# DMA transposes in place of TensorE transposes from the third group on, in a fused attention and MLP kernel

## The chip, the cores and the metric

The kernel runs on one core of one Trainium2 chip. The metric is device time in microseconds (us); the time before is 234.18 us, the median of three runs (233.75 to 235.13).

## What is computed

The input is q, k and v for 4 batches, 8 heads, 768 positions and a head dimension of 64, with one decay factor per head. Decayed linear attention gives a matrix of 3072 rows (batch and position) by 512 (head and head dimension), and an MLP follows, with the activation h times tanh(softplus(h)), called Mish. Cut to what matters:

```
for b in range(nb):                       # blocks of positions, in order
    intra = (qb @ kb.T) * Dmask           # lam ** (i - j) on and below the diagonal
    inter = (qb * lam_pow) @ kv_state
    out[b] = intra @ vb + inter
    kv_state = lam_block * kv_state + (kb * rev_pow).T @ vb
x = out as (batch * position, head * head_dim)      # 3072 x 512
h = x @ w_in                                        # 3072 x 2048
result = (h * tanh(softplus(h))) @ w_out            # 3072 x 512, float32
```

## The kernel before, in words

The positions are cut into NG = 6 groups of C = 128, numbered n = 0 to 5 here as in the code. A group holds one chunk of 128 positions of each of B = 4 batches; chunk i is batch i % 4 of group i // 4. Each chunk is worked on in two halves of four heads, so a group has eight halves.

**Attention of one half** is three pieces. `att_a` (L211) makes two transposes on TensorE: `pk` from the decayed k, `ktil` (L220, two matmuls of 128 columns against an identity), and `pq` from q (L223, two more). With group 1 and later it also issues `att_kv` (L187, two matmuls `pv` of 128 columns, k transposed times v) ahead of what follows. VectorE multiplies `pq` by the powers of the decay into `qT` (L230), and ScalarE copies `pk` into the zero-padded `kz` in two instructions of 64 partitions (L234). `att_w` (L200) updates the state of the half: VectorE adds (`raw`, L208), GpSimd multiplies (L209). `att_s` (L243) makes the scores `pS` in four matmuls (L248), and VectorE masks them into `sb` (L252). `att_o` (L255) makes `pO` from `sb`, v, and from group 1 on the state (L266, L270), and ScalarE copies it into `xt` (L273). The PSUM tiles pk, pq, pS and pO have one buffer each.

**The MLP of one group** is 32 units of four matmuls of 512 columns: 16 units `mm1_unit` (L316; `ph`, then Mish on ScalarE into `hsg`, L323), and 16 units `mm2_unit` (L327; `po`, four units for each chunk, then ScalarE copies to `osb`, L340, and SyncE (SP) issues the store, L342).

**The order** is written out by hand, and each engine runs its instructions in that order. The attention of group 0 comes first, alone. Loop n then emits the 32 units of group n's MLP with the 24 pieces of group n+1's attention between them: a0, a1, s0, then a, s, o of consecutive halves. In loop 0 the pieces stand four at a time after units 25 to 30 (units counted from 0); in loops 1 to 4 one piece stands after each unit from 7 to 30. Loop 5 has the MLP alone.

**Loads.** k, q and v are loaded from HBM and cast to 16 bits by DMAs that GpSimd (POOL) issues (L69, L73, L76), 128 KB of result each. `scale_k` (L174) multiplies k by its decay into `ktil`: on VectorE for group 0 and for chunk 8, on GpSimd for the others (L177). The weights are loaded between chunk 3 and chunk 4. The loads of group 2 (chunks 8 to 11) are issued at the end of loop 0, those of later groups in the second half of each chunk's `att_a`, one group ahead.

Of the kernel before, what the change touches and what calls it, by code (L numbers as in the profile page):

```python
# [21 lines left out]
def kernel(  # L22
# [10 lines left out]
    nc = tc.nc  # L33
    B, H, S, D = q.shape
    C = 128
    NG = S // C
    JP = H // 2
# [5 lines left out]
    MID = C // 2 - 1  # L43
    NVB = 8
    NKB = 4

    ctx.enter_context(tc.manual_schedule())
# [7 lines left out]
    qn = [None] * (NG * B)  # L55
# [7 lines left out]
    def load_k(i):  # L63
        if i < 2:
            kn[i] = const.tile([128, H, D], F32, name=f"kn{i}")
            nc.sync.dma_start(out=kn[i], in_=chunk_rows(k, i))
            return
        kn[i] = loads.tile([128, H, D], F16, name="kn", tag="kn")
        nc.gpsimd.dma_start(out=kn[i], in_=chunk_rows(k, i))  # L69
# [26 lines left out]
    def load_chunk(i):  # L96
        load_k(i)
        load_q(i)
        load_v(i)
# [54 lines left out]
    for hp in range(2):  # L154
        rs = slice(64 * hp, 64 * hp + 64)
# [3 lines left out]
    lq = const.tile([128, JP, C], F32, name="lq")  # L159
# [9 lines left out]
    ktil = {}  # L169

    class Half:
        pass

    def scale_k(i):  # L174

        t = work.tile([128, H, D], F16, name="ktil", tag="ktil", bufs=6)
        (nc.vector if i < B or i == 2 * B else nc.gpsimd).tensor_tensor(  # L177
            out=t, in0=kn[i], in1=bc(lk, 2, D), op=ALU.mult)
        ktil[i] = t


    wst = [
# [4 lines left out]
    def att_kv(s, spare):  # L187

        n, b, hf = s.n, s.b, s.hf
        i = n * B + b  # L190
        pv = ps.tile([128, 2, 128], F32, name="pv", tag=spare, bufs=2)
        for p in range(2):
            j = 2 * hf + p
            nc.tensor.matmul(  # L194
                pv[:, p, :].rearrange("p (a e) -> p a e", a=2), s.kp[p],
                vz[i % NVB][:, 2 * j : 2 * j + 2, 0:D], start=True, stop=True,
            )
        s.pv = pv

    def att_w(s):  # L200
        n, b, hf = s.n, s.b, s.hf
        w_new = wst[b][hf][(n + 1) % 2]
        lb = lbm[:, 2 * hf : 2 * hf + 2, :]
        if n == 0:
            nc.vector.tensor_tensor(out=w_new, in0=s.pv, in1=lb, op=ALU.mult)
        else:
            raw = work.tile([128, 2, 128], F32, name="raw", tag="raw", bufs=3)
            nc.vector.tensor_tensor(out=raw, in0=s.pv, in1=wst[b][hf][n % 2], op=ALU.add)  # L208
            nc.gpsimd.tensor_tensor(out=w_new, in0=raw, in1=lb, op=ALU.mult)  # L209

    def att_a(s):  # L211

        n, b, hf = s.n, s.b, s.hf
        i = n * B + b
        pk = ps.tile([128, 2, C], F32, name="pk", tag="pk")
        pq = ps.tile([128, 2, C], F16, name="pq", tag="pq")
        s.kp = [ktil[i][:, 4 * hf + 2 * p : 4 * hf + 2 * p + 2, :].rearrange("p h c -> p (h c)")
              for p in range(2)]
        for p in range(2):
            nc.tensor.matmul(pk[:, p, :], s.kp[p], ident, start=True, stop=True)  # L220
        for p in range(2):
            j = 2 * hf + p
            nc.tensor.matmul(  # L223
                pq[:, p, :], qn[i][:, 2 * j : 2 * j + 2, :].rearrange("p h c -> p (h c)"),
                ident, is_transpose=True, start=(p == 0), stop=(p == 1),
            )
        if 0 < n < NG - 1:
            att_kv(s, s.spare)
        s.qT = work.tile([128, 2, C], F16, name="qT", tag="qT", bufs=5)
        nc.vector.tensor_tensor(out=s.qT, in0=pq, in1=lq[:, 2 * hf : 2 * hf + 2, :], op=ALU.mult)  # L230
        s.kz = kz[s.seq % NKB]
        for hp in range(2):
            rs = slice(64 * hp, 64 * hp + 64)
            nc.scalar.activation(s.kz[rs, :, hp, :], pk[rs], AF.Copy)  # L234
        if n > 0:
            if n < NG - 1:
                att_w(s)
            if hf == 0 and i + 1 < s.loaded:
                scale_k(i + 1)
            if hf == 1 and n > 1 and i + B < NG * B:  # L240
                load_chunk(i + B)

    def att_s(s):  # L243

        psS = ps.tile([128, 4, C], F32, name="pS", tag="pS")
        for p in range(2):
            for hp in range(2):
                nc.tensor.matmul(  # L248
                    psS[:, 2 * p + hp, :], s.kz[:, p, hp, :], s.qT[:, p, :], start=True, stop=True,
                )  # L250
        s.sb = work.tile([128, 4, C], F16, name="sb", tag="sb", bufs=4)
        nc.vector.tensor_tensor(  # L252
            out=s.sb, in0=psS, in1=bc(maskT, 1, 4), op=ALU.mult)

    def att_o(s):  # L255

        n, b, hf = s.n, s.b, s.hf
        i = n * B + b
        if xt[n] is None:
            xt[n] = work.tile([128, JP, GT], F16, name="xt", tag="xt", bufs=2)  # L260
        psO = ps.tile([128, 2, C], F32, name="pO", tag="pO")
# [81 lines left out]


    scale_k(0)
    first_halves = att_halves(0)
    nh = len(first_halves)
# [17 lines left out]
    for hp in range(2):  # L365
        rs = slice(64 * hp, 64 * hp + 64)
        nc.vector.tensor_copy(lbm[rs, :, rs], bc(lbc[rs, :], 2, D))
    for n in range(NG):
        units = [(mm1_unit, (n, ni)) for ni in range(NKI)]
        units += [(mm2_unit, (n, b, part)) for b in range(B) for part in range(WS)]  # L370
        pieces = []
        if n + 1 < NG:
            pieces = att_pieces(n + 1)

        first = 24 if n == 0 else len(units) - 2 - len(pieces)
        room = len(units) - 2 - first
        per = len(pieces) / max(room, 1)
        for u, (fn, args) in enumerate(units):
            fn(*args)
            if n == 0 and 2 <= u < 2 + nh:  # L380
                att_kv(first_halves[u - 2], "po")
                att_w(first_halves[u - 2])
            if u == first - 3 and pieces:
                scale_k((n + 1) * B)
            left = len(units) - 2 - u
            while pieces and u >= first and len(pieces) > per * left:
                f2, s = pieces.pop(0)
                s.spare = "po" if u < NKI - 1 else "ph"
                f2(s)
        for f2, s in pieces:  # L390
            f2(s)
        if n == 0:
            for i in range(2 * B, 3 * B):
                load_chunk(i)


# [28 lines left out]
```

## Time and profile before

| | before |
|---|---|
| median of three runs | 234.18 us |
| the profiled execution's own time | 233.51 us |
| its span, first to last instruction | 231.7 us |
| granted TensorE clock | 1.000 |
| TensorE matmuls busy | 220.0 us (95%) |
| weight loads, beside the matmuls | 120.8 us (52%) |
| VectorE / ScalarE / GpSimd busy | 74.8 / 128.0 / 111.5 us |

The profiled execution is 1.81 us longer than its span and 0.67 us shorter than the median. Matmuls overlap in the trace: a matmul of 512 columns is shown with 379 ns, but four of them start within 0.86 us. So durations on TensorE are read from the starts of consecutive rows, not from busy time. The chain of work that ended last names, at each moment, what the end of the program depended on.

### The profile page before, as it was taken

The page shows a single profiled execution, that of the slowest core. Times are in us where ns is not written, and L with a number is a line of the kernel's source. Part 1 is how long each engine was busy: PE and PEld are TensorE (multiplying, and loading weights), DVE is VectorE, ACT ScalarE, POOL GpSimd, SP SyncE. Part 2 cuts the span into 40 slices and gives each one's busy share as a digit, 9 for nine tenths or more (in the row PEclk, how much of TensorE's full clock was granted, in tenths as well). Part 3 has the DMA queues.
Part 4 walks back from the last instruction along what each step waited for, and adds up shares of the span by engine and source line. Part 5 has one row for each costly group of instructions (what it writes and reads, how often), then busy time and mean ns, then how long its engine had stood idle before and what let it go on. Part 6 is the DMA issues. An engine that isn't in the chain of part 4 may idle for free.

```text
span 231.7 us, 3918 instructions
## 1 busy us (share of the span) xinstructions
PE 220.0 (95%) x1541; PEld 120.8 (52%) x1541; DVE 74.8 (32%) x159; ACT 128.0 (55%) x275; POOL 111.5 (48%) x139
## 2 busy tenths in 40 slices
PE   7797999789899999999999999999999999999993
PEld 2474544466445555545555545555545555544441
DVE  7784410277215443014433114433103323100000
ACT  5884662355577553477554477544478554476121
POOL 7992435766999865219865309865800000000000
PEclk9999999999999999999999999999999999999999
DMA  7999999921999978906988905998900011200112
GB/s 114 137 163 206 205 206 159 194 42 36 102 168 98 77 88 91 152 0 43 75 91 94 156 0 37 73 97 94 155 3 3 0 45 51 89 0 3 45 52 84
DMA packets 82722, 20.44 MB, mean 88 GB/s; under 512 B 75536, under 2 KB 79632, under 8 KB 82704
## 3 DMA queue, kind: packets, MB, share of 16 engines
q0 software_dynamic: 77024, 13.37, 73.3%
q1 hardware_dynamic: 5680, 6.82, 8.3%
q8 instruction: 12, 0.20, 0.4%
q14 instruction: 6, 0.05, 0.1%
HBM read 27.27 MB, written 6.29 MB: 145 GB/s over the span
## 4 chain that ended last, share of the span: by engine, by line
PE 77%; DMA 9%; POOL 7%; ACT 3%; issue 2%; DVE 1%; POOLq 0%; ACTq 0%
PE po L334 35%; PE ph L311 28%; DMA wout_84<-in_moe_w_out_dram 9%; PE pS L248 4%; PE pO L270 3%; PE pk L220 2%; PE pO L266 2%; PE pq L223 1%; POOL qn L73 1%; ACT kz_151 L234 1%; PE pv L194 1%; ACT hsg L323 1%; POOL kn L69 1%; DVE sb L252 1%; ACT xt L273 1%
## 5 line engine op out<-in xcount | busy, mean ns | idle before, releaser
L323 ACT ACTIVATE hsg<-ph 128x512 f16<-128x512 f32 x96 | 57.2, 597 | 25.1 <-PE ph L311 24.8
L334 PEld LDWEIGHTS <-hsg 128*128 128x128 f16 x384 | 34.6, 98 | 29.1 <-issue 0.5
L230 DVE TENSOR_TENSOR qT<-pq,lq 128x256 f16<-128x256 f16 x48 | 20.3, 424 | 90.3 <-PE pq L223 90.1
L252 DVE TENSOR_TENSOR sb<-pS,maskT 128x512 f16<-128x512 f32 x48 | 33.1, 689 | 22.4 <-PE pS L248 22.2
L273 ACT ACTIVATE xt<-pO 128x256 f16<-128x256 f32 x48 | 18.4, 382 | 31.3 <-PE pO L270 31.0
L340 ACT ACTIVATE osb<-po 128x512 f32<-128x512 f32 x24 | 14.3, 597 | 28.8 <-PE po L334 28.6
L73 POOL DMA_DIRECT2D qn<-in_q_dram x24 | 21.7, 905 | 6.9 <-DMA win_78<-in_moe_w_in_dram 2.8
L334 PE MATMUL po<-wout_84,hsg 128*128 128x512 f16 x96 | 24.6, 379 | 0.2 <-DMA wout_84<-in_moe_w_out_dram 0.2
L334 PE MATMUL po<-wout_81,hsg 128*128 128x512 f16 x96 | 24.6, 379 | 0.0
L334 PE MATMUL po<-wout_82,hsg 128*128 128x512 f16 x96 | 24.6, 379 | 0.0
L334 PE MATMUL po<-wout_83,hsg 128*128 128x512 f16 x96 | 24.6, 379 | 0.0
L311 PE MATMUL ph<-xt,win_79 128*128 128x512 f16 x96 | 23.9, 379 | 0.0
L311 PE MATMUL ph<-xt,win_80 128*128 128x512 f16 x96 | 23.7, 379 | 0.0
L311 PE MATMUL ph<-xt,win_77 128*128 128x512 f16 (+2 forms) x104 | 22.2, 363 | 1.1 <-DMA win_77<-in_moe_w_in_dram 0.6
L69 POOL DMA_DIRECT2D kn<-in_k_dram x22 | 20.4, 929 | 5.2 <-DMA win_77<-in_moe_w_in_dram 1.9
L311 PE MATMUL ph<-xt,win_78 128*128 128x512 f16 x96 | 22.0, 379 | 0.0
L177 POOL TENSOR_TENSOR ktil<-kn,lk 128x512 f16<-128x512 f16 x19 | 19.9, 1057 | 0.0
L220 PEld LDWEIGHTS <-ktil 128*128 128x128 f16 x96 | 9.2, 98 | 15.7 <-issue 5.2
L220 PE MATMUL pk<-ident,ktil 128*128 128x128 f16 x96 | 13.3, 221 | 3.9 <-ACT kz_151 L234 1.7
L311 PEld LDWEIGHTS <-win_77 128*128 128x128 f16 x104 | 9.7, 98 | 11.7 <-DMA win_77<-in_moe_w_in_dram 0.8
L311 PEld LDWEIGHTS <-win_78 128*128 128x128 f16 x96 | 9.2, 98 | 10.4
L223 PE MATMUL pq<-ident,qn 128*128 128x128 f16 x96 | 13.3, 220 | 0.0
(167 smaller groups left out, 268.5 us busy)
## 6 DMA issues: line engine op xcount, KB each, us to landing
out_dram<-osb SPq DMA_DIRECT2D x24, 256.0 KB, 2.0
qn<-in_q_dram POOLq DMA_DIRECT2D x24, 128.0 KB, 4.8
kn<-in_k_dram POOLq DMA_DIRECT2D x22, 128.0 KB, 3.7
win_77<-in_moe_w_in_dram POOLq DMA_DIRECT2D x1, 512.0 KB, 7.6
win_78<-in_moe_w_in_dram POOLq DMA_DIRECT2D x1, 512.0 KB, 10.1
win_79<-in_moe_w_in_dram POOLq DMA_DIRECT2D x1, 512.0 KB, 12.0
win_80<-in_moe_w_in_dram POOLq DMA_DIRECT2D x1, 512.0 KB, 13.7
wout_81<-in_moe_w_out_dram POOLq DMA_DIRECT2D x1, 512.0 KB, 15.5
```

The source lines that it names most:

```text
L69: nc.gpsimd.dma_start(out=kn[i], in_=chunk_rows(k, i))
L73: nc.gpsimd.dma_start(out=qn[i], in_=chunk_rows(q, i))
L177: (nc.vector if i < B or i == 2 * B else nc.gpsimd).tensor_tensor(out=t, in0=kn[i], in1=bc(lk, 2, D), op=ALU.mult)
L220: nc.tensor.matmul(pk[:, p, :], s.kp[p], ident, start=True, stop=True)
L223: nc.tensor.matmul(pq[:, p, :], qn[i][:, 2 * j : 2 * j + 2, :].rearrange("p h c -> p (h c)"), ident, is_transpose=True, start=(p == 0), st ...
L230: nc.vector.tensor_tensor(out=s.qT, in0=pq, in1=lq[:, 2 * hf : 2 * hf + 2, :], op=ALU.mult)
L252: nc.vector.tensor_tensor(out=s.sb, in0=psS, in1=bc(maskT, 1, 4), op=ALU.mult)
L273: nc.scalar.activation(dst, psO, AF.Copy)
L311: nc.tensor.matmul(ph_t[ni][:, lo:hi], win[ni // w][:, kc, (ni % w) * 128 : (ni % w) * 128 + 128], xt[n][:, kc, lo:hi], start=(kc == 0), s ...
L323: nc.scalar.activation(hsg[n][:, ni, :], ph_t.pop(ni), AF.Mish)
L334: nc.tensor.matmul(po, hsg[n][:, ki, b * C : (b + 1) * C], wout[part][:, kk, :], start=(ki == 0), stop=(ki == NKI - 1),)
L340: nc.scalar.activation(osb, po, AF.Copy)
```

## The change

From group 2 on (`NT = 2`), TensorE no longer transposes. A new function `turn(i)` scales chunk i's k as before and has SP issue two DMA transposes of a whole chunk, both from SBUF to SBUF: of q into `qraw` and of `ktil` into `kraw`, four buffers each. `att_a` then reads these: VectorE makes `qT` out of `qraw`, and VectorE, not ScalarE, copies `kraw` into `kz`. The PSUM of pk and pq, free now, gives pS and pO a second buffer each. `scale_k` of chunk 8 goes from VectorE to GpSimd.

The times at which things are issued move too. The pieces of group 1's attention stand thinner in loop 0, from unit 22 on instead of 25 (a table gives the pieces after each unit). In the later loops they stand one unit earlier, from unit 6 on. Eight of the twelve loads of group 2 are issued one at a time, one in each `att_a` of group 1; the other four, and `turn(8)`, follow at the end of loop 0. At the start of each later loop `turn` is called for the next group's second chunk, and from loop 2 on for its first; the third and fourth follow in the first halves of the first and second chunk.

```diff
+    def turn(i):
+        scale_k(i)
+        for src, name, to in ((qn, "qraw", qraw), (ktil, "kraw", kraw)):
+            to[i] = work.tile([128, JP, C], F16, name=name, tag=name, bufs=4)
+            nc.sync.dma_start_transpose(out=to[i], in_=src[i].rearrange("p h c -> p (h c)"))
+    ahead = [
+        (lambda f=f, i=i: f(i)) for i in range(2 * B, 3 * B) for f in (load_k, load_q, load_v)
+    ]
...
+        if n >= NT:
+            if n < NG - 1:
+                att_kv(s, s.spare)
+            nc.vector.tensor_tensor(
+                out=s.qT, in0=qraw[i][:, 2 * hf : 2 * hf + 2, :], in1=lqh, op=ALU.mult)
+            for hp in range(2):
+                rs = slice(64 * hp, 64 * hp + 64)
+                nc.vector.tensor_copy(s.kz[rs, :, hp, :], kraw[i][rs, 2 * hf : 2 * hf + 2, :])
+            if n < NG - 1:
+                att_w(s)
+            if hf == 0 and i + 2 < s.loaded:
+                turn(i + 2)
+            if hf == 1 and i + B < NG * B:
+                load_chunk(i + B)
+            return
...
         if n > 0:
-            if n < NG - 1:
-                att_w(s)
             if hf == 0 and i + 1 < s.loaded:
                 scale_k(i + 1)
-            if hf == 1 and n > 1 and i + B < NG * B:
-                load_chunk(i + B)
+            att_w(s)
+            ahead.pop(0)()
...
-        psS = ps.tile([128, 4, C], F32, name="pS", tag="pS")
+        psS = ps.tile([128, 4, C], F32, name="pS", tag=("pS", "pk")[s.seq % 2 if s.n >= NT else 0])
...
-        first = 24 if n == 0 else len(units) - 2 - len(pieces)
+        if n == 0:
+            room = dict(zip(range(22, 31), (1, 1, 2, 3, 3, 4, 4, 4, 2)))
+            if n > 0 and pieces and u == 0:
+                if n > 1:
+                    turn((n + 1) * B)
+                turn((n + 1) * B + 1)
...
         if n == 0:
-            for i in range(2 * B, 3 * B):
-                load_chunk(i)
+            turn(2 * B)
+            while ahead:
+                ahead.pop(0)()
```

On TensorE, this is the second half of chunk 8 (group 2) in loop 1, before the change. Rows name the line, the operation, and out<-in; the number behind a name tells buffers apart.

```order
L220 LDWEIGHTS ktil_953
L220 MATMUL pk_1003<-ident_87,ktil_953 128x128
L220 LDWEIGHTS ktil_953
L220 MATMUL pk_1003<-ident_87,ktil_953 128x128
L223 LDWEIGHTS qn_910
L223 MATMUL pq_1004<-ident_87,qn_910 128x128
L223 LDWEIGHTS qn_910
L223 MATMUL pq_1004<-ident_87,qn_910 128x128
L194 LDWEIGHTS ktil_953
L194 MATMUL pv_1009<-vz0_69,ktil_953 128x128
L194 LDWEIGHTS ktil_953
L194 MATMUL pv_1009<-vz0_69,ktil_953 128x128
```

The same half on TensorE with the change, with the matmul rows of the MLP on both sides of it (line 205 is line 194 of before, line 341 is line 311).

```order
L341 LDWEIGHTS win1_78
L341 MATMUL ph_999<-xt_693,win1_78 128x512
L205 LDWEIGHTS ktil_922
L205 MATMUL pv_1006<-vz0_69,ktil_922 128x128
L205 LDWEIGHTS ktil_922
L205 MATMUL pv_1006<-vz0_69,ktil_922 128x128
L341 LDWEIGHTS win2_79
L341 MATMUL ph_1020<-xt_693,win2_79 128x512
```

Four matmuls and four weight loads of the half are gone, and the piece now stands one unit earlier.

GpSimd during group 1's attention in loop 0, before: `ktil` of chunks 4 to 7 alternates with the state updates `w`, and the loads of group 2 begin behind the last of them.

```order
L177 TENSOR_TENSOR ktil_600<-kn_129,lk_179 128x512
L209 TENSOR_TENSOR w000_196<-raw_635,lbm_195 128x256
L177 TENSOR_TENSOR ktil_638<-kn_134,lk_179 128x512
L209 TENSOR_TENSOR w010_198<-raw_653,lbm_195 128x256
L209 TENSOR_TENSOR w100_200<-raw_676,lbm_195 128x256
L177 TENSOR_TENSOR ktil_679<-kn_139,lk_179 128x512
L209 TENSOR_TENSOR w110_202<-raw_714,lbm_195 128x256
L209 TENSOR_TENSOR w200_204<-raw_752,lbm_195 128x256
L177 TENSOR_TENSOR ktil_755<-kn_144,lk_179 128x512
```

The same place on GpSimd with the change, up to the same `ktil` of chunk 7.

```order
L181 TENSOR_TENSOR ktil_584<-kn_129,lk_179 128x512
L181 TENSOR_TENSOR ktil_619<-kn_134,lk_179 128x512
L220 TENSOR_TENSOR w000_196<-raw_621,lbm_195 128x256
L70 DMA kn_624<-in_k_dram 128x8x64
L220 TENSOR_TENSOR w010_198<-raw_646,lbm_195 128x256
L74 DMA qn_649<-in_q_dram 128x8x64
L181 TENSOR_TENSOR ktil_676<-kn_139,lk_179 128x512
L220 TENSOR_TENSOR w100_200<-raw_678,lbm_195 128x256
L77 DMA vz0_69<-in_v_dram 128x8x64
L220 TENSOR_TENSOR w110_202<-raw_715,lbm_195 128x256
L70 DMA kn_718<-in_k_dram 128x8x64
L181 TENSOR_TENSOR ktil_752<-kn_144,lk_179 128x512
```

Chunk 5 is scaled one place earlier, and four loads of group 2 stand ahead of the scaling of chunk 7; four more follow, and then the scaling of chunk 8. On SP, where before only the 24 stores followed the first loads, the order is now: the four stores of group 0, the eight transposes of group 2 (q, then k, for each chunk), the four stores of group 1, the eight transposes of group 3, and so on; the eight stores of groups 4 and 5 come last.

More of the change, by code (lines that the diff above doesn't have):

```diff
@@ L45 @@
     NKB = 4
+    NT = 2
     ctx.enter_context(tc.manual_schedule())
@@ L172 @@
         pass
+    kraw = {}
+    qraw = {}
     def scale_k(i):
         t = work.tile([128, H, D], F16, name="ktil", tag="ktil", bufs=6)
-        (nc.vector if i < B or i == 2 * B else nc.gpsimd).tensor_tensor(
+        (nc.vector if i < B else nc.gpsimd).tensor_tensor(
             out=t, in0=kn[i], in1=bc(lk, 2, D), op=ALU.mult)
         ktil[i] = t
+    def turn(i):
[3 more added lines that the diff above has]
+            nc.sync.dma_start_transpose(out=to[i], in_=src[i].rearrange("p h c -> p (h c)"))
     wst = [
@@ L214, in att_a @@
         i = n * B + b
+        lqh = lq[:, 2 * hf : 2 * hf + 2, :]
+        s.qT = work.tile([128, 2, C], F16, name="qT", tag="qT", bufs=5)
+        s.kz = kz[s.seq % NKB]
+        s.kp = [ktil[i][:, 4 * hf + 2 * p : 4 * hf + 2 * p + 2, :].rearrange("p h c -> p (h c)")
+                for p in range(2)]
+        if n >= NT:
[13 more added lines that the diff above has]
+            return
         pk = ps.tile([128, 2, C], F32, name="pk", tag="pk")
         pq = ps.tile([128, 2, C], F16, name="pq", tag="pq")
-        s.kp = [ktil[i][:, 4 * hf + 2 * p : 4 * hf + 2 * p + 2, :].rearrange("p h c -> p (h c)")
-              for p in range(2)]
         for p in range(2):
@@ L373 @@
             pieces = att_pieces(n + 1)
-        first = 24 if n == 0 else len(units) - 2 - len(pieces)
-        room = len(units) - 2 - first
-        per = len(pieces) / max(room, 1)
+        if n == 0:
+            room = dict(zip(range(22, 31), (1, 1, 2, 3, 3, 4, 4, 4, 2)))
+        else:
+            room = {u: 1 for u in range(len(units) - 2 - len(pieces), len(units) - 2)}
         for u, (fn, args) in enumerate(units):
@@ L382 @@
                 att_w(first_halves[u - 2])
[L383 to L386, printed above, removed]
+            if n == 0 and u == 18:
+                scale_k(B)
+            if n > 0 and pieces and u == 0:
+                if n > 1:
+                    turn((n + 1) * B)
+                turn((n + 1) * B + 1)
+            for _ in range(room.get(u, 0)):
                 f2, s = pieces.pop(0)
```

10 lines of the change are left out of this document (3 added, 7 removed).

## Prediction

> **What bounds the kernel now.** I read the page first, for the share of each engine and for the chain that ended last.
>
> ```profile
> span 231.7 us, 3918 instructions
> PE 220.0 (95%) x1541; PEld 120.8 (52%) x1541; DVE 74.8 (32%) x159; ACT 128.0 (55%) x275; POOL 111.5 (48%) x139
> PE 77%; DMA 9%; POOL 7%; ACT 3%; issue 2%; DVE 1%; POOLq 0%; ACTq 0%
> ```
>
> TensorE (PE) is busy nearly throughout and holds 77% of the chain; no other engine passes 55%. The share is an average, so I took the chain in order of time next (start, duration, what).
>
> ```profile
> 16.75 20.95 DMA wout_84<-in_moe_w_out_dram
> ...
> 60.55 6.92 PE ph L311 x32
> ...
> 95.64 6.92 PE ph L311 x32
> ...
> 165.81 6.92 PE ph L311 x32
> ...
> 200.11 13.81 PE ph L311 x64
> ```
>
> Until 16.75 + 20.95 = 37.7 us the last weight load sets the pace. From there the chain is TensorE's. The rows "ph L311 x32" mark where loops 1, 2 and 4 begin: loop 1 lasts 95.64 - 60.55 = 35.09 us, loop 4 200.11 - 165.81 = 34.30, and the last MLP 231.7 - 200.11 = 31.6. Those 32 matmuls are eight units of the MLP, so a unit is 6.92 / 8 = 0.865 us. To see whether a loop has room, I read the timeline of TensorE where loop 3 comes to the first two halves of group 4's attention.
>
> ```profile
> 137.47 0.28 PE L220 MATMUL pk<-ident,ktil 128*128 128x128 f16 x2
> 137.58 0.28 PE L223 MATMUL pq<-ident,qn 128*128 128x128 f16 x2
> 137.69 0.28 PE L194 MATMUL pv<-vz_69,ktil 128*128 128x128 f16 x2
> 137.80 1.03 PE L311 MATMUL ph<-xt,win_79 128*128 128x512 f16 x4
> 138.98 0.27 PE L220 MATMUL pk<-ident,ktil 128*128 128x128 f16 x2 [0.15 <-ACT kz_151 L234]
> ```
>
> Each pair of 128-column matmuls delays the next start by 0.11 us, so one costs 0.055. A loop with state updates then needs 32 x 0.865 + 8 x 16 x 0.055 = 27.7 + 7.0 = 34.7 of its 35.1 us: loops 1 to 4 are streams of matmuls with holes of 0.4 us. What is taken off TensorE there comes off the time, unless something else is late.
>
> **The transposes taken off TensorE.** Groups 2 to 5 lose 4 groups x 8 halves x 4 matmuls = 128, at 0.055 us: 7.04 us. The weight loads that go with them run beside matmuls.
>
> **A wait that goes with them.** The last row above starts at 138.98, though the unit before it ends at 137.80 + 0.86 = 138.66: the second half's `pk` waits 0.32 us for ScalarE to empty the only buffer. That is about the 0.4 us missing above, once in each of four loops: 1.28 us. With the change the half begins with `pv`, which has two buffers. What is late next is VectorE, which empties them.
>
> ```profile
> L230 DVE TENSOR_TENSOR qT<-pq,lq 128x256 f16<-128x256 f16 x48 | 20.3, 424 | 90.3 <-PE pq L223 90.1
> L252 DVE TENSOR_TENSOR sb<-pS,maskT 128x512 f16<-128x512 f32 x48 | 33.1, 689 | 22.4 <-PE pS L248 22.2
> L208 DVE TENSOR_TENSOR raw<-pv,w_210 128x256 f32<-128x256 f32 x2 | 0.8, 415 | 0.0
> L156 DVE COPY lnp<-lnb 64x4 f32<-64x4 f32 x2 | 0.5, 245 | 0.6 <-ACT lnb L149 0.5
> L367 DVE COPY lbm<-lbc 64x256 f32<-64x256 f32 x2 | 0.9, 471 | 0.1
> ```
>
> VectorE gains two copies of 64x256 a half. No row has them from SBUF in 16 bits; the copies shown bound them at 245 and 471 ns, and the larger shape is the nearer. A half then costs VectorE at most 0.42 + 0.94 + 0.42 + 0.69 = 2.5 us, against 3 units and 12 small matmuls on TensorE, 3.25 us. So they hide, and without that cover each half would cost what is over. ScalarE loses its two copies, which were off the path. GpSimd's extra `scale_k` of chunk 8 stands behind group 1's attention.
>
> **The transposes as DMAs.** No DMA in this trace transposes, so I bound them. The first two are from the DMA view of 57 to 72 us, when loads run at full rate; the others are the page's, and SP's timeline where loop 1 begins.
>
> ```profile
> q0 software_dynamic: 12465, 1.57, 164.5%
> ...
> out_dram<-osb SPq DMA_DIRECT2D x1, 256.0 KB, 4.5
> ...
> q1 hardware_dynamic: 5680, 6.82, 8.3%
> out_dram<-osb SPq DMA_DIRECT2D x24, 256.0 KB, 2.0
> ...
> 61.21 0.33 SPq L342 DMA_DIRECT2D out_dram<-osb  x1
> ```
>
> Occupancy first. SP's queue moved 6.82 MB in 8.3% of 231.7 us, so 128 KB at that rate takes 0.37 us. The loads moved 12465 packets in 15 us, 831 a microsecond; a load of 128 KB with rows of 64 elements has 128 x 8 = 1024 of them, so 1.23 us. Were a transpose cut into 65536 pieces of 2 bytes at the same packet rate, it would be 79 us. I take 0.4 to 1.2, because the order shows one DMA for each 128x512 block, as for a load. A loop's 8 transposes, 12 loads and 4 stores are then at most 9.6 + 14.8 + 3.0 = 27.4 us of some 33: the DMA engines keep up.
>
> Latency next. A store lands 2.0 us after its issue, 4.5 among loads. Take chunk 12, whose transposes stand behind the last store of loop 1. That store is issued 61.21 - 60.55 = 0.66 us after a loop begins and holds SP 0.33 us; q's transpose then holds SP by 0.33 to about 1.2 us (its occupancy), and k's lands 2.0 to 4.5 us after its issue, so 3.3 to 6.7 us after the loop began. It is needed by s0, behind units 0 to 8 and two `pv` pairs, 9 x 0.865 + 0.22 = 8.0, less `qT` and the two copies, 1.36: 6.6 us. So it is in time by 3.3 us or late by 0.1; I take in time. In loops 2 to 4 the second chunk has those five units more, the third and fourth are asked for nine units or more ahead of their first piece. The q transposes wait only for loads that landed a loop before. What is queued behind a waiting transpose on SP is transposes, and then the stores of the group, which begin 13 units later. GpSimd, whose `ktil` the k transposes wait for, is free where loops 2 to 4 begin. In loop 1 it still issues group 2's loads: by the rows of the next part chunk 8's `ktil` ends 7.8 us (four `w`, four loads, one scaling) after chunk 7's, at 61.7, and chunk 9's 4.9 us later, at 66.6. Loop 1 begins at 59.7, so chunk 8 lands by 4.0 to 6.5 us in, with 6.6 allowed, and chunk 9 by 8.9 to 11.4, with 11.9 allowed (s2 stands five units and 1.0 us of pieces behind s0).
>
> **The first attention in loop 0.** Here TensorE has holes. First its rows, then GpSimd's.
>
> ```profile
> 41.20 1.03 PE L334 MATMUL po<-wout_84,hsg 128*128 128x512 f16 x4
> ...
> 43.78 0.27 PE L220 MATMUL pk<-ident,ktil 128*128 128x128 f16 x2
> ...
> 53.81 0.27 PE L220 MATMUL pk<-ident,ktil 128*128 128x128 f16 x2
> ```
>
> ```profile
> 42.37 1.08 POOL L177 TENSOR_TENSOR ktil<-kn,lk 128x512 f16<-128x512 f16 x1
> 45.04 0.73 POOL L209 TENSOR_TENSOR w_196<-raw,lbm 128x256 f16<-128x256 f32 x1 [1.59 <-DVE raw L208]
> ...
> 52.56 1.05 POOL L177 TENSOR_TENSOR ktil<-kn,lk 128x512 f16<-128x512 f16 x1
> 57.53 0.95 POOL L69 DMA_DIRECT2D kn<-in_k_dram  x1
> ```
>
> From 43.78 to 60.55 TensorE has 6 units and 24 pieces, 5.2 + 7.0 = 12.2 us of work in 16.8. With the change a0 stands behind unit 22, at 41.20. Chunk 4's `ktil` still ends at 42.37 + 1.08 = 43.45, since the loads of group 1 stand ahead of it on GpSimd; TensorE idles 2.3 us and owes three more units, 2.6 us. It gets them back from the holes up to a6, which needs chunk 7's `ktil`. GpSimd now reaches that by 45.04 + 4 x 0.73 + 4 x 0.95 + 2 x 1.05 = 53.9, against 52.56 + 1.05 = 53.6. So a6 starts at about 53.9, as it does now (53.81), and from it on stand three units, 2.6 us, and a6 to o7, 48 small matmuls, 2.6: 5.2 us, where it now takes 60.55 - 53.81 = 6.7. Some holes stay: o7 waits for ScalarE to empty the one pO, a7's scores for its copies. I allow 0.7 us and take a gain of 0.8. Bounds: 1.5 if no hole stays, a loss of 1 if the loads and `w` reach a6 two places later.
>
> **The sum**, on the profiled execution: 233.51 - 7.04 - 1.28 - 0.8 = 224.4 us. The median stood 0.67 above it: 225.1 us.
>
> **The rivals.**
>
> Transposes go one at a time, and SP's queue becomes the bound (slower). Mechanism: 32 transposes with a price T each, from 60.4 us on, and each waits for the one before it. The last must be there for a6 of loop 4; behind that stand 0.9 us of VectorE, 10 units and 36 small matmuls, 10.6 us, and the last MLP, 31.6. The span is 60.4 + 32 T + 43.1, which passes 231.7 from T = 4.0 us on. By the landing time of the store among loads, 4.5, the span is 247.5 and the time 247.5 + 1.81 + 0.67 = 250 us. For it: nothing here shows a transpose. Against: a store's transfer and landing, 0.37 and 2.0, lie far below 4.0. Chance 0.15, the case of 79 us each (2.6 ms in all) within it.
> The Trainium skill (VectorE: DVE Perf Modes, "The three transpose paths") has a 128x128 transpose of 16 bits at 390 ns on TensorE and 1309 ns by DMA, and so speaks against the change. Four such blocks in a row are an estimate of 5.2 us for one of these DMAs; by that rule the span would be 270 us. No run here shows it, and TensorE's 0.055 us for such a block against the page's 390 ns shows that its figures are not prices in a stream.
>
> The first chunk of each group is late, or loop 0 loses. If `kraw` lands 1.3 us late in four loops, 5.2 us of the gain go: 230.3. If GpSimd's interleaved loads push a6 by 2 us, it is 227. Both still gain. Chance 0.11.
>
> The matmuls were covered anyway (no change, 234.2). TensorE would have to wait elsewhere for the same time, on VectorE above all. Against: it shows 2.5 us a half against 3.25, and the loops have 0.4 us of holes. Chance 0.06.
>
> **How the numbers follow.** No change means within 0.5% (1.2 us), which is about what a measurement of this kernel can tell. The forecast, 223.3 to 227.5, has 0.68; with the late cases faster has 0.79, same 0.06, slower 0.15. The range goes from 223.3 (loop 0 gains 0.7 more, the loops lose their last 0.1 us of holes each, and the run stands as far below its median as the profiled one did, 0.7) to 231.5, the late case with 1.2 us of scatter, and leaves out the last two, 0.2.
>
> **What would show it.** In the new profile loops 1 to 3 should last about 33.0 us and loop 4 about 32.2; loop 1 should begin at about 59.7; DVE's `qT` from `qraw` should wait for TensorE's order of work or nothing, not for a DMA. A row of VectorE or TensorE that waits for `kraw` or `qraw` at a loop's start for more than its slack, or SP with transposes back to back over a loop, proves me wrong, and the sign then hangs on T against 4.0 us.

## The result, and the profile after

The changed kernel takes 228.02 us (median of 4 runs, 227.86 to 228.25) against 233.97 us for the kernel before, in runs on the same chip: a ratio of 0.974, 95% interval 0.970 to 0.977. That is 2.6% faster, where 3.9% was forecast; 2.9 us of the forecast gain are missing. The profiled execution took 227.86 us, 5.65 less than that of before.

The page of the changed kernel, its span, the busy time of the engines and the shares of the chain:

```profile
span 226.0 us, 3703 instructions
...
PE 211.8 (94%) x1413; PEld 113.0 (50%) x1413; DVE 99.6 (44%) x222; ACT 105.8 (47%) x211; POOL 113.5 (50%) x140
...
PE 73%; DMA 12%; POOL 9%; DVE 2%; issue 1%; SPq 1%; ACT 1%; POOLq 0%; ACTq 0%; DVEq 0%
```

128 matmuls are gone (1541 to 1413), ScalarE is 22 us less busy and VectorE 25 us more. The share of DMA in the chain has grown from 9% to 12%: a transfer has come onto the path. The chain in order of time shows which (start, duration, what):

```profile
61.75 1.30 SPq L190
63.18 7.01 DMA kraw<-ktil
72.24 0.98 DVE kz_152 L243
...
96.32 6.04 PE ph L341 x28
...
129.30 6.04 PE ph L341 x28
...
162.29 7.77 PE ph L341 x36
...
194.38 13.81 PE ph L341 x64
```

The new link is one transpose, `kraw` of chunk 8 at the start of loop 1, with 7.01 us from issue to landing. Behind it the chain is TensorE's alone. The rows "ph L341" mark where loops 2, 3 and 4 and the last MLP begin (the chain puts these starts 0.16 to 0.17 us later than TensorE's timeline does): loop 2 lasts 129.30 - 96.32 = 32.98 us, loop 3 32.99, loop 4 32.09. TensorE's timeline shows the places where it stood still, first in loop 0, then in loop 1:

```profile
43.63 0.28 PE L254 MATMUL pk<-ident,ktil 128*128 128x128 f16 x2 [2.12 <-POOL ktil L181]
...
53.64 0.28 PE L254 MATMUL pk<-ident,ktil 128*128 128x128 f16 x2
...
57.30 0.38 PE L278 MATMUL pS<-qT,kz_154 128*128 128x128 f16 x4 [0.78 <-DVE sb L282]
...
59.36 0.22 PE L296 MATMUL pO<-qT,w_211 128*128 128x128 f16 x1 [0.47 <-ACT xt L303]
...
60.55 3.62 PE L341 MATMUL ph<-xt,win_77 128*128 128x512 f16 x16
...
67.68 1.03 PE L341 MATMUL ph<-xt,win_79 128*128 128x512 f16 x4
70.56 0.60 PE L278 MATMUL pS<-qT,kz_151 128*128 128x128 f16 x4 [1.84 <-DVE kz_151 L243]
70.99 1.03 PE L341 MATMUL ph<-xt,win_79 128*128 128x512 f16 x4
...
72.83 0.22 PE L278 MATMUL pS<-qT,kz_152 128*128 128x128 f16 x1
73.27 0.34 PE L278 MATMUL pS<-qT,kz_152 128*128 128x128 f16 x3 [0.22 <-DVE kz_152 L243]
```

The unit at 67.68 ends at 68.55, and s0 starts at 70.56: 2.0 us late, with 0.2 more in the slow `pS` itself and 0.4 at the next half's `kz_152`. That is 2.6 us, and loop 1 lasts 35.6 us where 33.0 were forecast. The table has, from the profiled execution of each kernel below, when the last weight load lands (its issue plus its time to landing), where loop 1 begins on TensorE's timeline, and how long the loops are.

| kernel | last weight load lands | loop 1 begins | loop 1 | loop 2 | loop 3 | loop 4 |
|---|---|---|---|---|---|---|
| before | 37.70 | 60.39 | 35.08 | 35.09 | 35.08 | 34.31 |
| changed | 37.85 | 60.55 | 35.60 | 32.99 | 32.99 | 32.09 |
| e1 late loads | 37.36 | 60.07 | 32.99 | 32.98 | 32.99 | 32.09 |
| e2 copies on ScalarE | 37.20 | 59.91 | 37.26 | 33.69 | 33.69 | 33.19 |
| e3 single pS and pO | 37.72 | 60.44 | 36.63 | 32.99 | 32.98 | 32.09 |
| e4 loop 0's table alone | 37.68 | 60.74 | 35.09 | 35.08 | 35.09 | 34.31 |
| e5 loop 0 early | 37.17 | 60.43 | 32.99 | 32.99 | 32.98 | 32.10 |
| e6 loads together | 36.91 | 59.62 | 36.20 | 32.99 | 32.98 | 32.09 |
| e7 third group on TensorE | 37.73 | 60.45 | 35.09 | 32.99 | 32.98 | 32.09 |
| e8 transposes twice | 37.29 | 60.00 | 35.78 | 33.18 | 32.98 | 32.10 |
| e9 loop 0 early, later table | 37.20 | 57.99 | 32.99 | 32.99 | 32.99 | 32.09 |
| e10 late loads again | 36.52 | 59.23 | 32.99 | 32.99 | 32.98 | 32.10 |

Loops 2 to 4 give 2.10 + 2.09 + 2.22 = 6.4 us; loop 1 takes 0.5 back and its start 0.2: 5.7 us, which is the difference of the two profiled executions (5.65). The start of loop 1 scatters with the last weight load, and a difference of 0.2 us there says nothing by itself. Counted from that landing, loop 1 begins 22.69 us later in the kernel before, and 22.70 in the changed kernel (22.70 to 22.72 in all eight versions with its table for loop 0): loop 0 gained nothing and lost nothing. The question for the experiments is why neither loop 1 nor loop 0 gains anything.

### The profile page after: what moved, and what is told of

Its sections match the earlier page's. It is cut to its first block, busy times and chain, and to the rows that moved or that the text cites. A ratio compares the mean times of both kernels' runs of the same rounds, so it can differ in the third digit from the quotient of the medians.

```text
span 226.0 us, 3703 instructions
## 1 busy us (share of the span) xinstructions
PE 211.8 (94%) x1413; PEld 113.0 (50%) x1413; DVE 99.6 (44%) x222; ACT 105.8 (47%) x211; POOL 113.5 (50%) x140
## 4 chain that ended last, share of the span: by engine, by line
PE 73%; DMA 12%; POOL 9%; DVE 2%; issue 1%; SPq 1%; ACT 1%; POOLq 0%; ACTq 0%; DVEq 0%
PE po L364 34%; PE ph L341 26%; DMA wout_84<-in_moe_w_out_dram 9%; PE pS L278 4%; PE pO L300 4%; DMA kraw<-ktil 3%; PE pO L296 2%; POOL qn L74 2%; PE pv L205 1%; POOL kn L70 1%; DVE kz_152 L243 1%; DVE sb L282 1%; SPq L190 1%; ACT osb L370 1%; POOL ktil L181 0%
## 5 line engine op out<-in xcount | busy, mean ns | idle before, releaser
L239 DVE TENSOR_TENSOR qT<-qraw,lq 128x256 f16<-128x256 f16 x32 | 15.4, 481 | 30.7 <-DMA qraw<-qn 30.6
L341 PE MATMUL ph<-xt,win_77 128*128 128x512 f16 (+2 forms) x104 | 22.2, 363 | 1.5 <-DMA win_77<-in_moe_w_in_dram 1.1
L341 PE MATMUL ph<-xt,win_79 128*128 128x512 f16 x96 | 23.6, 379 | 0.0
L341 PE MATMUL ph<-xt,win_80 128*128 128x512 f16 x96 | 23.3, 379 | 0.0
L341 PE MATMUL ph<-xt,win_78 128*128 128x512 f16 x96 | 22.4, 379 | 0.0
L181 POOL TENSOR_TENSOR ktil<-kn,lk 128x512 f16<-128x512 f16 x20 | 20.9, 1067 | 0.1
L341 PEld LDWEIGHTS <-win_77 128*128 128x128 f16 x104 | 9.7, 98 | 12.1 <-DMA win_77<-in_moe_w_in_dram 1.2
L341 PEld LDWEIGHTS <-win_78 128*128 128x128 f16 x96 | 9.1, 98 | 9.7
L263 DVE TENSOR_TENSOR qT<-pq,lq 128x256 f16<-128x256 f16 x16 | 6.7, 421 | 16.3 <-PE pq L257 16.2
L341 PEld LDWEIGHTS <-win_80 128*128 128x128 f16 x96 | 8.8, 98 | 7.8
L341 PEld LDWEIGHTS <-win_79 128*128 128x128 f16 x96 | 8.7, 98 | 7.3
```

The costliest lines, as they stand in the source:

```text
L181: (nc.vector if i < B else nc.gpsimd).tensor_tensor(out=t, in0=kn[i], in1=bc(lk, 2, D), op=ALU.mult)
L239: nc.vector.tensor_tensor(out=s.qT, in0=qraw[i][:, 2 * hf : 2 * hf + 2, :], in1=lqh, op=ALU.mult)
L341: nc.tensor.matmul(ph_t[ni][:, lo:hi], win[ni // w][:, kc, (ni % w) * 128 : (ni % w) * 128 + 128], xt[n][:, kc, lo:hi], start=(kc == 0), s ...
```

## The experiments

Theory A: in loop 1 the transposes of chunk 8 run among the last loads of group 2, and those make them late. Theory B: VectorE, which has the copies now, is the limit there. Theory C: loop 0's new table gains nothing because the wait for the first `ktil` only takes the place of later holes. Experiments e1, e2, e5, e9 and e10 were run 4 to 10 times each; e3, e4 and e6 to e8 are one execution each and are read from their loops.

**e1, the last four loads of group 2 later** (theory A)

```diff
+    late = [ahead.pop(-3), ahead.pop(-2), ahead.pop(-2), ahead.pop(-1)]
...
+            if late:
+                late.pop(0)()
+                if i == 2 * B and hf == 0:
+                    late.pop(0)()
...
-            while ahead:
-                ahead.pop(0)()
```

They are issued in the first three halves of loop 1's attention instead of ahead of it, 7 to 12 us later, and the transposes of chunk 11 one chunk later.

> The last four loads of group 2 (k and q of chunk 11, v of chunks 10 and 11) are issued in the first three halves of loop 1's attention instead of at the end of loop 0, and chunk 11 is turned two halves later; all else as in the changed kernel. Theory A (loop 1 is 2.6 us too long because chunk 8's transposes land late among the loads, 7.0 us after issue against a median of 2.5): kraw of chunk 8 lands 3 to 4.5 us after its issue, the 1.84 us wait of pS on kz disappears, loop 1 falls from 35.6 to 33.0 to 33.6 us and the time from 228.0 to about 225.6 to 226. Theory B (VectorE's copies of kraw, up to 0.98 us each where the median is 0.22, make kz late): the copies stay as slow, loop 1 stays above 35 us and the time at 228.

Measured: 225.15 us (224.75 to 227.25), a ratio of 0.966 (0.961 to 0.972) to before. The view of the tile `kraw` has the landing times of all transposes of k, here in the changed kernel:

```profile
DMA to landing us min/median/max: 2.4/2.5/7.0
```

The same tile in e1:

```profile
DMA to landing us min/median/max: 2.4/2.4/4.1
```

The median hardly moves; the longest landing falls from 7.0 to 4.1 us. The DMA view of 60 to 70 us says what stood beside chunk 8's transposes (a queue's packets, MB and share; for each issue KB and median us to landing; q0 is the software queue, with the loads that GpSimd issues). The changed kernel:

```profile
q0 software_dynamic: 5635, 0.71, 116.9%
...
qraw<-qn SPq DMA_TRANSPOSE x3, 5.5
kraw<-ktil SPq DMA_TRANSPOSE x2, 5.9
```

The same view of e1:

```profile
q0 software_dynamic: 1058, 0.13, 20.9%
...
qraw<-qn SPq DMA_TRANSPOSE x3, 2.5
kraw<-ktil SPq DMA_TRANSPOSE x3, 2.5
```

With the loads' packets cut from 5635 to 1058 in those 10 us, the median transpose takes 2.5 us instead of 5.5 to 5.9. Chunk 8's k is issued at the same point of the loop in both kernels (63.18 - 60.55 = 2.63 and 62.73 - 60.07 = 2.66 us in), so it is the landing alone that differs. No wait is left on TensorE in loop 1 of e1, which lasts 32.99 us, as loops 2 and 3 do. Theory A accounts for the whole 2.6 us. It also speaks against theory B: the copies are still VectorE's, and still take up to 1.12 us.

**e2, the copies into `kz` on ScalarE** (theory B)

```diff
-                nc.vector.tensor_copy(s.kz[rs, :, hp, :], kraw[i][rs, 2 * hf : 2 * hf + 2, :])
+                nc.scalar.activation(s.kz[rs, :, hp, :], kraw[i][rs, 2 * hf : 2 * hf + 2, :], AF.Copy)
```

> From group 2 on ScalarE, not VectorE, copies kraw into kz; all else as in the changed kernel. Theory A (latency of the DMA): kraw of chunk 8 lands as late as before and the time stays within 0.5 us of 228.0; loop 1 loses at most the 0.3 to 0.4 us that the second half's copies cost. Theory B (slow copies on VectorE beside GpSimd's work): loop 1 falls by 1 us or more, to 34.6 or less, and the time to 227 or less. Either way VectorE's busy time falls by some 27 us, and its qT rows of 0.57 us go back to 0.42.

Measured: 232.34 us (230.82 to 234.22), a ratio of 0.996 (0.993 to 0.999): 4.3 us slower than the changed kernel by the medians of their two sets of runs, 4.2 by the four loops. No theory had that. ScalarE's timeline in loop 1:

```profile
69.48 0.85 ACT L243 ACTIVATE kz<-kraw 64x256 f16<-64x256 f16 x2 [2.73 <-DMA kraw<-ktil]
70.36 0.60 ACT L353 ACTIVATE hsg<-ph 128x512 f16<-128x512 f32 x1
```

And TensorE's:

```profile
67.04 1.03 PE L341 MATMUL ph<-xt,win 128*128 128x512 f16 x4
69.95 0.23 PE L278 MATMUL pS<-qT,kz 128*128 128x128 f16 x1 [1.89 <-ACT kz L243]
70.39 0.46 PE L278 MATMUL pS<-qT,kz 128*128 128x128 f16 x3 [0.21 <-ACT kz L243]
71.01 1.86 PE L341 MATMUL ph<-xt,win 128*128 128x512 f16 x4 [0.16 <-ACT hsg L353]
```

TensorE comes to s0 2.05 us late (67.04 + 0.86 to 69.95), as in the changed kernel (2.0): the wait for chunk 8 is the same with the copies on either engine. In the changed kernel s0 starts 0.37 us after the landing (63.18 + 7.01 = 70.19), so VectorE's copies account for no more than that of its 2.0. Theory B falls, although loop 1 is 1.7 us longer, which theory A did not expect either. The rows show where those 1.7 us come from. On ScalarE the first `hsg` that stands behind the copy, whose `ph` was ready at about 68.1, starts at 70.36, since the copy ahead of it waited 2.73 us for the transpose; TensorE loses about 0.5 us between 70.39 and 71.01, the end of it waiting for that `hsg`. The changed kernel lost 0.2 there. Most of the 1.7 us is a lower clock. TensorE by stretches, with its granted clock (PEclk):

```profile
core 0: us, PE busy (x), PEclk, DMA share, GB/s
...
70.00:75.00 5.00, 4.63 (x21) 0.66 1.23 114
```

The units at 71.01 and 72.88 take 1.66 and 1.36 us instead of 0.86: with the pair of `pv` between them 1.4 us. In the changed kernel the granted clock stayed at 1.00 there. In loops 2 and 3, at full clock, the copies cost 0.7 us a loop, in loop 4 1.1; in loop 2 the longest wait is one for `hsg` (0.36 us).

**e3, a single buffer for pS and pO**

```diff
-        psS = ps.tile([128, 4, C], F32, name="pS", tag=("pS", "pk")[s.seq % 2 if s.n >= NT else 0])
+        psS = ps.tile([128, 4, C], F32, name="pS", tag="pS")
-        psO = ps.tile([128, 2, C], F32, name="pO", tag=("pO", "pq")[s.seq % 2 if s.n >= NT else 0])
+        psO = ps.tile([128, 2, C], F32, name="pO", tag="pO")
```

> pS and pO keep one PSUM buffer each from group 2 on, as before; all else as in the changed kernel. If the second buffers carry part of the gain, loops 2 and 3 grow from 33.0 us by up to 0.3 us each, and more where VectorE's sb is late (its halves now take up to 3.8 us): up to 1 us a loop. If the holes of before came from the one pk buffer alone, loops 2 to 4 stay at 33.0, 33.0 and 32.1.

Measured: 228.79 us. Loops 2 to 4 are unchanged; loop 1 is 1.0 us longer, for one wait on TensorE's timeline:

```profile
74.14 0.38 PE L278 MATMUL pS<-qT,kz 128*128 128x128 f16 x4 [1.33 <-DVE sb L282]
```

The second buffers were worth something only here, where TensorE runs close behind a late VectorE.

**e4, the table of loop 0 alone** (theory C): the kernel before with the changed kernel's thinner table for loop 0; TensorE transposes throughout.

```diff
-        first = 24 if n == 0 else len(units) - 2 - len(pieces)
+        if n == 0:
+            room = dict(zip(range(22, 31), (1, 1, 2, 3, 3, 4, 4, 4, 2)))
...
```

> The kernel before with one part of the change: the thinner table of loop 0 (pieces from unit 22 on, scaling of chunk 4 emitted after unit 18); the loads of group 2 stay at the end of loop 0. Theory C (the idle time only moves, from the dense pieces to the wait for chunk 4's ktil at unit 22, and the tail s6, s7, o6, o7 keeps its holes for the single pS and pO): loop 1 begins at 60.1 to 60.6, as before (60.39) and after (60.55), and the time is within 0.5 us of before. Rival (the table gains the 0.8 us that was forecast, and the interleaved loads take it back): loop 1 begins at 59.4 to 59.8 and the time falls by 0.6 to 1.0 us.

Measured: 233.84 us, loop 1 from 60.74 us on, against 60.39 in the profile of before; from the last weight load it is 23.06 us, against 22.69. TensorE waits 1.74 us for the first `ktil` there, where the kernel before had no wait. (Of the 0.37 us more, 0.26 are a second wait, for chunk 5's `ktil`, which this version still scales late.) The table alone gains nothing, and theory C stands so far.

**e5, loop 0's attention earlier:** e1 with the first chunks of group 1 scaled as soon as their loads allow, and the pieces from unit 17 on.

```diff
-        (nc.vector if i < B else nc.gpsimd).tensor_tensor(
+        (nc.vector if i < B + 2 else nc.gpsimd).tensor_tensor(
...
-            room = dict(zip(range(22, 31), (1, 1, 2, 3, 3, 4, 4, 4, 2)))
+            room = dict(zip(range(17, 31), (1, 1, 1, 2, 2, 2, 2, 2, 2, 2, 2, 2, 2, 1)))
...
-            if n == 0 and u == 18:
-                scale_k(B)
+            if n == 0 and u == 15:
+                for i in range(B, 2 * B):
+                    scale_k(i)
```

> On top of the kernel with late loads (e1_loads_late): chunks 4 and 5 are scaled on VectorE, 6 and 7 on GpSimd, all four emitted after unit 15; the pieces of group 1's attention stand from unit 17 on, one or two after each unit; raw has six buffers instead of three. Theory C (loop 0 loses its time to TensorE's wait for chunk 4's ktil, which stands on GpSimd behind the loads of group 1, and to pieces too dense for the single pS and pO): TensorE runs loop 0 from unit 19 on (37.7 us) nearly without holes, 13 units and 128 small matmuls, 11.2 + 7.1 us, so loop 1 begins at 56 to 57.5 us instead of 60.1; loops 1 to 4 stay at 33.0, 33.0, 33.0 and 32.1; the time is 221 to 222.5. Rival (loop 0 is held by the loads of chunks 6 and 7, which land at 40 to 46 us, or by GpSimd's queue of state updates and loads): loop 1 begins at 59 or later and the time stays above 224.

Measured: 225.32 us (224.09 to 226.32), a ratio of 0.963 (0.959 to 0.967), no better than e1; loop 1 begins at 60.43, not at 56 to 57.5. A miss. VectorE's timeline has the first chunk's scaling:

```profile
38.03 0.69 DVE L181 TENSOR_TENSOR ktil<-kn,lk 128x512 f16<-128x512 f16 x1 [7.62 <-DMA kn<-in_k_dram]
```

TensorE's timeline at the first piece:

```profile
38.78 0.29 PE L261 MATMUL pk<-ident,ktil 128*128 128x128 f16 x2 [1.92 <-DVE ktil L181]
...
39.74 0.28 PE L205 MATMUL pv<-vz,ktil 128*128 128x128 f16 x2 [0.56 <-DMA vz<-in_v_dram]
39.86 1.81 PE L369 MATMUL po<-wout,hsg 128*128 128x512 f16 x4
```

And TensorE by stretches, with its granted clock (PEclk):

```profile
core 0: us, PE busy (x), PEclk, DMA share, GB/s
...
39.00:44.00 5.00, 4.45 (x25) 0.66 2.44 156
44.00:49.00 5.00, 5.00 (x48) 1.00 0.91 102
```

GpSimd issued this load of k at 19.6 us, but it landed at 38.0, behind the weights. TensorE was there first and waited twice, 2.8 us between the rows in all, and after that its granted clock was 0.66 over five microseconds: the unit at 39.86 takes 1.6 us instead of 0.86, and all the slow rows up to 43.6 cost 1.7. Starting five units earlier only ran TensorE into that wait and the low clock; behind them its rows show no hole of more than 0.1 us.

**e6, group 2's loads together:** all twelve are issued at the end of loop 0, the three of chunk 8 ahead of its scaling and the other nine right behind it.

```diff
-            ahead.pop(0)()
...
+            for _ in range(3):
+                ahead.pop(0)()
```

> One part of the change undone: the loads of group 2 are issued together at the end of loop 0, as before (chunk 8's three, then its turn, then the other nine), not spread over group 1's attention. Theory A (a transpose among loads lands 6 to 7 us after issue, and spreading the loads keeps most of the transposes out of them): kraw of chunk 8 lands at 69 us or later and chunk 9's at 73 or later, loop 1 grows from 35.6 to 37 to 41 us, the later loops stay at 33.0, 33.0, 32.1; the time is 229.5 to 234. Rival (spreading does not matter, chunk 8's lateness has another cause): loop 1 stays within 0.5 us of 35.6.

Measured: 227.41 us, loop 1 36.20 us. The longest landing of `kraw` is 6.5 us, no longer than in the changed kernel, although nine loads are issued beside chunk 8's transposes instead of four. Chunk 8's own loads come later here, so its k is issued 63.15 - 59.62 = 3.53 us into loop 1 instead of 2.63. The expected 37 to 41 us for loop 1 is a miss, and so is the rival's 35.1 to 36.1: spreading the loads is worth 0.6 us there. Whether loads run beside those transposes matters; how many hardly did in this one execution. Loop 1 begins 22.71 us after the last weight load here too, with none of these loads among group 1's pieces, so the loads that the change puts there do not take back a gain of the table (e4's rival).

**e7, the third group on TensorE too**

```diff
-    NT = 2
+    NT = 3
...
```

> NT = 3: group 2 too is transposed on TensorE, groups 3 to 5 by DMA; all else as in the changed kernel. By the price of the matmuls (32 of 0.055 us a group, and 0.3 us of waiting for pk) loop 1 lasts 35.1 us as before, loops 2 to 4 33.0, 33.0 and 32.1: half a microsecond less than the changed kernel, whose loop 1 lasts 35.6, and about 2 us more than with late loads. The time is 227 to 227.8.

Measured: 227.41 us, as expected. Loop 1 lasts 35.09 us, as before the change, and 2.10 more than loop 2: the price of one group's transposes on TensorE, with the wait for `pk` that comes with them.

**e8, every transpose twice**

```diff
+        for src in (qn, ktil):
+            more = work.tile([128, JP, C], F16, name="more", tag="more", bufs=4)
+            nc.sync.dma_start_transpose(out=more, in_=src[i].rearrange("p h c -> p (h c)"))
```

> Every transpose is issued a second time into a tile that nobody reads, behind the pair that is used; the result is the same. By the spacing of SP's issues (1.31 us) 16 transposes hold SP 21 us of a loop of 33. Theory (neither SP nor the DMA engines are near their limit, the price of a transpose in a stream is 1.3 us against the 4.0 us from which it decides): loops 2 to 4 stay within 0.3 us of 33.0, 33.0 and 32.1; loop 1, where chunk 9's transposes come 2.6 us later, may grow by 1 to 3 us. Rival (the DMA engines are nearly full with loads, stores and transposes): loops 2 to 4 grow by over 1 us each.

Measured: 228.02 us; loops 3 and 4 are unchanged and loop 2 0.2 us longer. SP's timeline in loop 2:

```profile
97.09 1.22 SPq L190 DMA_TRANSPOSE qraw<-qn  x1
98.42 1.21 SPq L190 DMA_TRANSPOSE kraw<-ktil  x1
99.68 1.26 SPq L193 DMA_TRANSPOSE more<-qn  x1
```

They follow each other by 1.3 us, so SP has room for 25 in a loop; the change needs 8. Loop 1, which might have grown by 1 to 3 us, grew by 0.2.

**e9 and e10, loop 0 once more.** e9 is e5 with the pieces from unit 20 on, and chunk 8's transposes issued within loop 0's attention; e10 is e1 again, beside it on the same chip.

```diff
+            if b == 2 and hf == 0:
+                turn(2 * B)
...
-            room = dict(zip(range(17, 31), (1, 1, 1, 2, 2, 2, 2, 2, 2, 2, 2, 2, 2, 1)))
+            room = dict(zip(range(20, 31), (1, 0, 1, 2, 3, 3, 3, 3, 3, 3, 2)))
...
-        if n == 0:
-            turn(2 * B)
```

> The version with the late loads, and in loop 0 the four chunks of group 1 are scaled ahead of everything (two on VectorE, two on GpSimd), as in the experiment before that moved the first attention forward; but the first piece now stands after unit 20 instead of 17, since the first scaled k and its v were there only at 38.7 and 39.7 us in that run, and the transposes of chunk 8 are issued inside loop 0, at half 4 of its attention. If what held loop 0 back there was only the wait of TensorE for the weights and the first load (1.9 + 0.6 us of idle time and some 2 us of slow matmuls after it), TensorE has 11 units and 24 pieces left at about 39.3 us, 9.5 + 7.0 = 16.5 us dense, so loop 1 begins at 56 to 57.5 us, and with loops of 33.0, 33.0, 33.0, 32.1 and the last MLP of 31.6 the span is 219 to 220.5 and the time 221 to 222.5. If the chain of k loads (38.0, 40.6, 43.3, 45.8 us for chunks 4 to 7) and VectorE's and GpSimd's work behind them set the pace of the attention, loop 1 begins at 59 to 60.5 again and the time stays at 225. If chunk 8's transposes, now issued among loads, land over 6.6 us into loop 1, loop 1 is 1 to 2 us longer: 223 to 224.

> The kernel with the last four loads of group 2 moved into loop 1, once more and beside the version above on the same chip: 225.2 us within 0.5, loop 1 33.0 us long. It separates what the version above gains in loop 0 from the scatter of the start, which moved the first piece of loop 0 by up to 0.9 us from run to run.

Measured: e9 223.07 us (222.59 to 223.33), a ratio of 0.953 (0.950 to 0.955) to before; e10 225.02 us (224.02 to 226.95), 0.964 (0.960 to 0.967). The intervals do not meet: e9 is the fastest version of the study, 4.7% under the kernel before. Its TensorE in loop 0:

```profile
39.35 0.28 PE L261 MATMUL pk<-ident,ktil 128*128 128x128 f16 x2
...
57.99 6.21 PE L348 MATMUL ph<-xt,win 128*128 128x512 f16 x28
```

The first piece starts without a wait, and loop 1 begins at 57.99, half a microsecond past the expected range. From a0 on TensorE had 11 units and 24 pieces, 9.5 + 7.0 = 16.5 us, in 57.99 - 39.35 = 18.6: holes of 2.1 us. In the changed kernel it had nine units, 7.8 + 7.0 = 14.8, in 60.55 - 43.63 = 16.9: the same 2.1, and 2.1 of waiting ahead of a0. In the kernel before it was 12.2 in 60.39 - 43.78 = 16.6: 4.4 of holes and no wait. So the change's table only turned 2.3 us of holes into 2.1 of waiting (theory C), and what e9 gains in loop 0 is that wait. The starts of loop 1 in e9 and e10, 57.99 and 59.23, understate it, because e9's last weight load landed 0.7 us later. From that landing e9's loop 1 begins 20.79 us later and e10's 22.71: a gain of 1.9 us, which is the difference of the two medians, 1.95.

## Why the prediction was right, and where not

**The transposes taken off TensorE, and the wait that goes with them.** Right. Loops 2 to 4 were forecast at 33.0, 33.0 and 32.2 us and came at 32.99, 32.99 and 32.09. Per loop 32 matmuls at 0.055 and the wait for `pk`, 1.76 + 0.32 = 2.08, stand against 2.10 by e7.

**VectorE as the next to be late.** Right in the result, wrong in the size. At most 2.5 us a half were forecast, with copies of 245 to 471 ns. The groups of two of the four `kz` in the changed kernel, 129 to 162 us, loop 3 (busy us, mean ns of one):

```profile
L243 DVE COPY kz_152<-kraw 64x256 f16<-64x256 f16 x4 | 2.8, 703 | 0.1
...
L243 DVE COPY kz_153<-kraw 64x256 f16<-64x256 f16 x4 | 1.3, 319 | 0.1
```

The same groups from 162 to 195 us, loop 4:

```profile
L243 DVE COPY kz_153<-kraw 64x256 f16<-64x256 f16 x4 | 0.9, 220 | 0.1
...
L243 DVE COPY kz_152<-kraw 64x256 f16<-64x256 f16 x4 | 0.9, 218 | 0.1
```

In loop 4, where GpSimd has nothing to do, a copy takes 0.22 us; in loops 1 to 3, where it scales and updates states, the mean of `kz_152` is 0.70 and the longest copy 1.12, over twice the 0.47 that was to be the most. In loop 2, by the starts of `qT` at 102.92, 105.98, 108.16, 111.75 and 113.93 us, a half takes VectorE 3.1 to 3.6 and 2.2 us in turn, 2.75 on average, still under TensorE's 3.25: the cover that the forecast named was thinner than it said, and held.
The Trainium skill (GPSIMD Engine Reference, "1. Specifications") says that GpSimd shares its SBUF interfaces with VectorE, with contention where VectorE's instruction runs in a two-port mode or has two SBUF inputs. The rows above fit it, though no row shows in which mode a copy runs, and no run here took GpSimd's work away on purpose: that GpSimd slows the copies is not shown.

**The transposes as DMAs: occupancy.** Right, at the upper end. SP was to be held 0.33 to 1.2 us by each. SP's timeline of the changed kernel, in loop 1 and then in loop 2:

```profile
61.38 0.33 SPq L372 DMA_DIRECT2D out_dram<-osb  x1
61.75 1.30 SPq L190 DMA_TRANSPOSE qraw<-qn  x1
63.18 1.61 SPq L190 DMA_TRANSPOSE kraw<-ktil  x1
...
97.46 1.22 SPq L190 DMA_TRANSPOSE qraw<-qn  x1
98.79 1.21 SPq L190 DMA_TRANSPOSE kraw<-ktil  x1
100.10 1.21 SPq L190 DMA_TRANSPOSE qraw<-qn  x1
```

It is held 1.2 us in loop 2 (1.3 and 1.6 among loop 1's loads), and the next follows after 1.31, far below the 4.0 us from which the serial rival decides; e8, with twice as many at no loss in loops 3 and 4, rules that rival out.
The Trainium skill (VectorE: DVE Perf Modes, "The three transpose paths") has 1309 ns for a 128x128 block by DMA, from which the prediction made 5.2 us for one of these. Here 1.31 us is the distance of two transposes of 128x512, so 0.33 us a block; the measurement decides, and 1309 ns is not the price of a block in a stream.

**The transposes as DMAs: latency.** This step failed: "k's lands 2.0 to 4.5 us after its issue", and for chunk 8 "lands by 4.0 to 6.5 us in, with 6.6 allowed". Alone a transpose lands in 2.4 us, near the lower end. Among four loads chunk 8's k took 7.0. The upper end came from the one store in the trace that ran beside loads; a store is another transfer, and one sample is no upper end. It landed 63.18 + 7.01 - 60.55 = 9.6 us into the loop, 3.0 after the time allowed; TensorE lost 2.6. Of the 3.1 us beyond the forecast's latest, 6.5, 2.5 are the landing; 0.6 are the issue, which came 2.63 us in, behind the store and q's transpose on SP, where chunk 8's `ktil` was taken to decide, at 2.0. By the prediction's own sign, a row that waits for `kraw` at a loop's start, loop 1 proves this step wrong. The rival of a late first chunk was this mechanism, at one place instead of four: 2.6 us instead of 5.2. Where loops 2 to 4 begin no loads run beside the transposes, and nothing is late.

**Loop 0.** The gain of 0.8 us did not come: from the last weight load to loop 1 it is 22.70 us, against 22.69 before, inside the bounds given (1.5 gained to 1 lost). The first steps were right: TensorE idles 2.1 us before a0 (2.3 forecast) and a6 starts at 53.64 (53.9). What failed is "I allow 0.7 us" for the holes behind a6. They are 0.9 us at 57.30, for the single `pS`, and 0.6 at 59.36, for the single `pO`: 1.7 with the small ones, so 6.9 us where 5.2 + 0.7 were forecast. In group 1 pS and pO still have one buffer each.

The sum missed the profiled execution by 227.86 - 224.4 = 3.5 us: 2.6 in loop 1, 0.8 in loop 0's gain, and 0.15 because the last weight load landed that much later than in the profile of before. The median, 228.02, lies beyond the 227.5 up to which the forecast without a late case went, in the part of the range that was kept for the late rival.

## What to carry to other kernels

Matmuls that stand in a dense stream are worth their issue distance, and that price held to a few hundredths of a microsecond; what has to be bounded well is the latency of the transfers that take their place, at the one moment when other transfers run beside them. Take that bound from the busiest stretch and leave a margin, or move the competing transfers: here four loads issued 7 to 12 us later were worth 2.6 us. To compare a stage between two executions, count from the event that starts it: here the landing of one load scattered by 1.3 us, and the stage behind it, in eight versions, by 0.02. When an engine starts earlier, ask which input is the last to arrive, since an early start only turns later holes into one wait, and an instruction that waits on an in-order engine holds up all that stands behind it.

## What was not expected of the hardware

- A DMA transpose of 128x512 elements of 16 bits lands 2.4 us after its issue. Among loads of the software queue (5635 packets in 10 us) the medians were 5.5 us (q) and 5.9 (k), with 7.0 for the longest.
- A copy of 64x256 on VectorE takes 0.22 us with GpSimd idle, and 0.3 to 0.7 on average, 1.12 at most, beside GpSimd's work.
- A load issued behind the weights lands behind them: 18 us from issue to landing in e5.
- After waits of 1.9 and 0.6 us within 3 us (e5), and of 1.9 and 0.2 us (e2), TensorE's granted clock was 0.66 over 5 us, and matmuls took up to twice as long. In the changed kernel it stayed at 1.00 after waits of 1.8 and 0.2 us within 3 us (70.5 to 75 us), and after a single one of 2.1 (43.6 to 48 us). What decides between the two stays open.
